# A scheduler's delays taken from the trace, and two batches' first-layer products by turns

## Chip, core and metric

The kernel runs on one core of a Trainium2 chip. The metric is the device time of one execution in microseconds. The engines: TensorE (PE) multiplies and, with an identity as one operand, transposes; VectorE (DVE), ScalarE (ACT) and GpSimd (POOL) work element by element; SyncE (SP) starts most transfers. [...]

## What is computed

```
# x: 8 batches, 8 heads, 512 tokens, 64;  state: 8, 8, 32, 64   (float32)
scores = x @ state^T / 8;   a  = softmax over the 32 states;   xread = a @ state
scores2 = state @ x^T / 8;  a2 = softmax over the 512 tokens;  sread = a2 @ x
y = concat([xread, sread], tokens)            # 8 x 544 tokens, heads side by side: 4352 rows of 512
h = y @ w_in                                  # w_in: 512 x 2048, float64
g = where(h > 0, h, exp(min(h, 0)) - 1)       # ELU
out = g @ w_out                               # w_out: 2048 x 512, float64
```

## The kernel before

All products are in float32. Three ideas matter here.

*Weights.* The weights arrive as 64-bit floats, in 32 blocks of 512 KB, sixteen for each layer. The chip makes 32-bit floats of them from the two words, with two passes on ACT and four on DVE for a block. The six buffers for raw blocks (`raws`) lie in the memory (`t_w_sb`) that later holds weight sums.

```python
def convert(dst, raw, pool_clamp=False, pool_add=False):
    lo, hi = words(raw)
    ...
    A.activation(out=lo.bitcast(FP32), in_=lo, func=AF.Copy, scale=2.0**-51, bias=2.0)
    A.activation(out=dst, in_=hi.bitcast(FP32), func=AF.Abs)
    (Q if pool_clamp else V).tensor_scalar(out=dst, in0=dst, ..., op0=ALU.max, op1=ALU.min)
    V.tensor_scalar(out=bits, in0=bits, scalar1=3, ..., op0=ALU.logical_shift_left)
    V.scalar_tensor_tensor(out=q, in0=hi, scalar=0x80000000, in1=lo, ...)
    (Q if pool_add else V).tensor_tensor(out=bits, in0=bits, in1=q, op=ALU.add)
```

*Order of work.* xread @ w_in is computed as a @ (state @ w_in). `make_m` is the inner product, for one of eight slices (`hc`) of w_in: 64 x 32 blocks of state times 256 columns of weights. `ffn1_plain` is the outer one, followed by the ELU: one ACT pass for exp, one for Relu, and one DVE operation. The converted slices of w_in are also stored in DRAM (`keep_w`); later batches fetch them again (`fetch`) into three buffers (`w_half`). The second layer, and for later batches the first too, use Strassen's scheme, whose sums of weights and of activations lie on DVE and POOL. `move_state` brings the second attention's weights into the form that `state_read` needs, with sixteen small transfers inside the chip's memory. `load_blocks` loads x of the next batch in blocks that DVE turns (`turn_blocks`).

```python
def start():
    ...
    load_states(0, 2, raw_s, (SP, ACT))
    load_x(0, (SP, ACT))
    ...
    for n in range(6):
        read_block(n)
    turn_states(raw_s, 0, 2)
    turn_x(ob)
    scores(0, ob)
    softmax(0, a_sb)
    for hc in range(8):
        for r in range(2):
            n = 2 * hc + r
            convert(*blocks[n])
            read_block(n + 6)
        ...
        make_m(0, hc, w)
        copy_m_half(0, hc, m_sb[:, c % 2])
        make_m(1, hc, w)
        dma(w_in_mem[:, hc], w, tokens=((), (f"mem{hc}",)), kind="keep_w")
        ...
        if hc == 2:
            turn_state()
            state_read(0)
            load_x(1)
            load_states(2, B, raw_t, (SP,))
            turn_states(raw_t, 2, B)
        if hc == 4:
            turn_x(ob)
            scores(1, ob)
            softmax(1, aT1)
            turn_state()
            state_read(1)
        if hc % 2:
            ffn1_plain(0, c, g0, a_sb, e_slots)
    for c in range(FC):
        ffn1_plain(1, c, g_sb, aT1, e_slots)
        for n in range(16 + 4 * c, 20 + 4 * c):
            convert(*blocks[n])
            if n + 6 < 32:
                read_block(n + 6)
    ...        # second layer of batch 0, then of batch 1; batches 2 to 7; the eight batches' sread rows
```

*The scheduler.* The code above runs no instruction at once: each call adds an operation, with an estimated cost, to a list. `Plan` then plays the list through, three times, against a model of the engines, [...]six rotating PSUM banks and the DMA queues. It keeps the order of its shortest pass, and the instructions of every engine are put out in that order. So the estimates set no time on the chip; they set the order. Where the model sees PE idle in the first 40 us, it puts in filler products of the identity, which keep PE running and whose result is used nowhere.

```python
class Plan:
    FREE_BANKS = 6
    LATENCY = {PE: 0.19, DVE: 0.07, ACT: 0.07, POOL: 0.09, SP: 0.0}
    ...
    def lag(self, a, b):
        return 0.0 if a.engine == b.engine and a.engine != SP else self.LATENCY[a.engine]
    ...
            _, n, op = heapq.heappop(heaps[e])       # PE: lowest number that is ready; others: earliest due
    ...
            if e == SP or op.moved:
                wire = max(wire, op.end) + op.moved / 260e3
                op.end = max(wire, op.end) + 1.9
...
def dma(out, in_, tokens=((), ()), queue=SP, kind="dma"):
    ...
    plan.add(
        queue, 0.06, issue(engine, "dma_start", dict(out=out, in_=in_)), [in_], [out],
        moved=size, tokens=tokens, name=kind,
    )
```

All instructions are put out by one helper (L410), so the profile tells them apart by tile and shape, not by line; the filler alone has its own line, L1341. In the tiles' names, `ps` is PSUM, `aT` the softmax weights, `m` the product of state and w_in, `g`, `sec` and `s` hold activations and their sums, `t_w` the raw blocks and then the weight sums, `xr` and `soft` the attention, `o` and `m` the output.

Of the kernel before, what the change touches and what calls it, by code (L numbers as in the profile page):

```python
# [76 lines left out]
class Op:  # L77
    __slots__ = (
        "number", "engine", "cost", "emit", "deps", "opens", "closes", "port", "moved", "start",
        "end", "due", "users", "name",  # L80
    )


class Plan:


    FREE_BANKS = 6
    LATENCY = {PE: 0.19, DVE: 0.07, ACT: 0.07, POOL: 0.09, SP: 0.0}
    WINDOW = 60

# [97 lines left out]
    def lag(self, a, b):  # L188
        return 0.0 if a.engine == b.engine and a.engine != SP else self.LATENCY[a.engine]

    def set_due(self, after):
        at = 0.0
        for op in self.ops:
            op.due = 1e6 + op.number
            if op.engine == PE:
                op.due = at
                at += op.cost
        follow = {}
        for a, b in after:
            follow.setdefault(a, []).append(b)  # L200
        for op in reversed(self.ops):
            took = op.cost
            if op.engine == SP:
                took = 2.0 + op.moved / 250e3
            for u in op.users:
                op.due = min(op.due, u.due - self.lag(op, u) - took)
            for u in follow.get(op, ()):
                op.due = min(op.due, u.due - self.lag(op, u) - took)

    def run(self, filler=None, until=0.0):  # L210
# [10 lines left out]
        next_bank, opened, port, wire = 0, 0.0, 0.0, 0.0  # L221
        holder, after, done, fills = {}, [], [], []
        left = [op for op in self.ops if op.engine == PE]
        lowest = 0

# [28 lines left out]
        while count < len(self.ops):  # L254
# [14 lines left out]
            if e == PE:  # L269
                while left and left[0] in scheduled:  # L270
                    left.pop(0)
                if heaps[e][0][1] > left[0].number + 1200:
                    assert pending[e] or True
            _, n, op = heapq.heappop(heaps[e])
            if op.port and port > at + 1e-9:
# [11 lines left out]
                heapq.heapify(heaps[e])  # L287
                op = x[2]
            op.start, op.end = at, at + op.cost
            if e == PE and filler and at < until:  # L290
                gap = op.start - free_at[PE]
# [18 lines left out]
            for b in self.closing.get(op, ()):  # L310
                if b.fixed is None:
                    lag = 0.0 if op.engine == PE else self.LATENCY[op.engine]
                    heapq.heappush(open_banks, (op.end + lag, b.index))
                    holder[b.index] = op
# [24 lines left out]
def kernel(  # L339
# [78 lines left out]
    class Engine:  # L418
# [3 lines left out]
        def __getattr__(self, name):  # L422
            def call(**kw):
# [5 lines left out]
                if self.key == DVE:  # L429
                    cost = 0.07 + 1.042 * n  # L430
                    alone = len(wide) == 1 and not isinstance(kw["out"], View)
                    if alone and name in ("tensor_scalar", "tensor_copy"):
                        cost, port = 0.07 + 0.65 * n, n > 0.1
                    port = port or len(wide) > 1
                elif self.key == ACT:
                    cost = 0.093 + 0.833 * n
                    cost += 0.09 * sum(is_ap(kw[k]) for k in ("scale", "bias") if k in kw)
                else:
                    cost = 0.1 + (2.45 if len(wide) > 1 else 1.85) * n
                    port = True  # L440
# [9 lines left out]
    def products(cost, calls, name="mm"):  # L450
# [15 lines left out]

        plan.add(PE, cost, emit, ins, outs, name=name)

    def turns(cost, calls, name="turn"):
# [9 lines left out]

        plan.add(PE, cost, emit, ins, outs, name=name)  # L480

# [30 lines left out]

    def x_tokens():
        return xe.rearrange("p (r c) -> p r c", r=R)

    def load_x(b, queues=(SP,)):
        x_v = x[b].rearrange("h (p r) d -> p r h d", r=R)
        for r in range(R):
            dma(
                x_tokens()[:, r].rearrange("p (h d) -> p h d", d=D), x_v[:, r],  # L520
                queue=queues[r % len(queues)], kind="load_x",
            )

    def load_blocks(b, raw):
# [16 lines left out]

    def turn_x(to):

        for i in range(2):
# [3 lines left out]
            for j in range(2):  # L548
                for r in range(R):
                    m = 2 * i + j  # L550
                    calls += turn_calls(
                        [v[t][:, j, r] for t in range(2)], x_tokens()[:, r, m * P : (m + 1) * P]
                    )
            turns(1.3, calls, "turn_x")
            o = to[:, i * 1024 : (i + 1) * 1024].rearrange(
# [5 lines left out]
    def load_states(b0, b1, raw, queues):  # L561
        for c in range(G):
            for m in range(NP):
                dma(
                    raw[m * NS : (m + 1) * NS, :, c], state_v[c, m, :, b0:b1],
                    queue=queues[(c * NP + m) % len(queues)], kind="load_states",
                )

    def turn_states(raw, b0, b1):
# [8 lines left out]
        turns(0.15 * n, calls, "turn_states")  # L578
        o = kT[:, b0:b1].rearrange("p b (t q) -> p t b q", t=2)
# [14 lines left out]
    def scores(b, xT):  # L594
        st[b, "s"] = ps = [bank(), bank()]
        by_state(
            b, ps, [xT[:, m * 512 : (m + 1) * 512] for m in range(NP)], slice(0, 512), 0.95,
            name="scores",
# [7 lines left out]
    def make_m(b, hc, w):  # L606
        c, h = divmod(hc, 2)
        if h == 0:
            st[b, "m", c] = [bank(), bank()]
        by_state(  # L610
            b, st[b, "m", c], [w[:, m] for m in range(NP)], slice(h * 256, (h + 1) * 256), 0.48,
            start=h == 0, name="make_m",
# [101 lines left out]

    def state_read(b):
        ps = bank()
        calls = []
        for g in range(G):
            for r in range(R):
                for m in range(NP):  # L720
                    calls.append((
                        ps[m * NS : (m + 1) * NS, g * D : (g + 1) * D],
                        read_weights()[:, g, r, m * NS : (m + 1) * NS],
                        x_tokens()[:, r, m * P + g * D : m * P + (g + 1) * D],
                        dict(start=r == 0, stop=r == R - 1, tile_position=(0, m * NS)),
                    ))
        products(1.1, calls, "state_read")
        for g in range(G):
# [306 lines left out]
    def start():  # L1035
# [3 lines left out]
        raw_s = g_flat[:, : 2 * P].rearrange("p (b c d) -> p b c d", b=2, c=G)  # L1039
        raw_t = g_flat[:, 2 * P : 8 * P].rearrange("p (b c d) -> p b c d", b=6, c=G)  # L1040
        m1 = [g_flat[:, (c + 1) * 2048 : (c + 1) * 2048 + 1024] for c in range(3)]
        m1.append(w_half[:, 2].rearrange("p m k -> p (m k)"))
        aT1 = s_buf[:, :1024]

        load_states(0, 2, raw_s, (SP, ACT))
        load_x(0, (SP, ACT))
        blocks = {}

# [3 lines left out]
        for n in range(6):  # L1052
            read_block(n)
        turn_states(raw_s, 0, 2)
        turn_x(ob)
        scores(0, ob)
        softmax(0, a_sb)
        for hc in range(8):
            for r in range(2):
# [8 lines left out]
            dma(w_in_mem[:, hc], w, tokens=((), (f"mem{hc}",)), kind="keep_w")  # L1068
            if hc % 2 == 0 or c < 3:
                copy_m_half(1, hc, m1[c] if c < 3 else None) if c < 3 else None  # L1070
            if hc == 7:
                copy_m(1, 3, m1[3])
            if hc == 2:
                turn_state()
                state_read(0)
                load_x(1)
                load_states(2, B, raw_t, (SP,))
                turn_states(raw_t, 2, B)
            if hc == 4:
                turn_x(ob)  # L1080
                scores(1, ob)
                softmax(1, aT1)
                turn_state()
                state_read(1)
            if hc % 2:
                ffn1_plain(0, c, g0, a_sb, e_slots)
        for c in range(FC):
            ffn1_plain(1, c, g_sb, aT1, e_slots)
            for n in range(16 + 4 * c, 20 + 4 * c):
                convert(*blocks[n])  # L1090
                if n + 6 < 32:
                    read_block(n + 6)
        n0 = Strassen(2, g0, [m_sb[:, i, :1024] for i in range(2)], s_buf)
# [27 lines left out]
        softmax(2, a_sb)  # L1121
        load_x(2)
        o.product(x1, o.s, t_w[1], False)
# [10 lines left out]
    def ffn2(o, b, x1=None):  # L1134
# [4 lines left out]
        if six:  # L1139
# [12 lines left out]
            if nxt:  # L1152
                softmax(b + 1, a_sb)
                load_x(b + 1)
                move_state()
# [61 lines left out]
    def turn_read():  # L1217
# [7 lines left out]
        turns(1.3, calls, "turn_read")  # L1225
        xT = st["xT"] = xr[:, :1024].rearrange("p (m b s) -> p m b s", m=NP, b=B)
# [156 lines left out]
```

## Time and profile before

| what | value |
|---|---|
| time, median of 3 runs | 754.21 us (752.23 to 756.72) |
| span of the profiled run | 752.6 us |
| PE, DVE, ACT, POOL busy | 96, 73, 39, 17% of the span |
| DMA moved | 78.52 MB, mean 104 GB/s |
| fetches of stored slices (512 KB) | 56, median 4.4 us from issue to landing |
| small moves for state_read (32 KB) | 96, median 1.9 us |
| x in blocks (64 KB) | 80, median 2.7 us |

A row of a group gives line, engine, operation, output and input tiles, shapes, how many, then busy time in us and mean ns of one, then the idle time before it and what ended it. A float32 product stands in the trace as two records. "SPq" is the issuing of a transfer by SyncE: while it lasts, nothing else on that queue is issued. The granted clock is 1.00 where TensorE runs at full speed.

### The profile page before, as it was taken

How to read it: one execution, taken by the hardware profiler on the slowest of the kernel's cores; microseconds unless marked ns; L12 is line 12 of the kernel's file. 1: busy time of each engine (PE TensorE's matmuls, PEld its weight loads, DVE VectorE, ACT ScalarE, POOL GpSimd, SP SyncE). 2: the span in 40 equal slices, each digit the busy share in tenths (PEclk: the TensorE clock that was granted, in tenths of full speed). 3: DMA queues.
4: the chain of work that ended last, by engine and by line, in shares of the span. 5: the costliest groups of instructions: out<-in, count | busy, mean ns of one | idle time of the engine just before them, and what ended most of it. 6: DMA issues, size and time to landing. Idle time of an engine off the chain costs nothing.

```text
span 752.6 us, 14169 instructions
## 1 busy us (share of the span) xinstructions
PE 725.4 (96%) x5608; PEld 593.3 (79%) x5608; DVE 548.7 (73%) x1030; ACT 295.6 (39%) x576; POOL 128.2 (17%) x158
## 2 busy tenths in 40 slices
PE   9998999999989989998999999998999899999998
PEld 7643458888968878787977888777978797899887
DVE  2997999998557956896858875895679684887231
ACT  4798991012056121732065213722074206610220
POOL 1101000042111150305130341107030522000000
PEclk9999999999999999999999999999999999999999
DMA  8797650223251343524172135324262323000401
GB/s 239 218 282 261 204 169 27 57 51 105 76 142 63 58 128 84 140 57 125 46 193 60 27 115 130 109 51 133 73 153 57 90 71 140 11 1 29 141 29 28
DMA packets 133442, 78.52 MB, mean 104 GB/s; under 512 B 114432, under 2 KB 114944, under 8 KB 133376
## 3 DMA queue, kind: packets, MB, share of 16 engines
q1 hardware_dynamic: 130880, 76.96, 36.4%
q10 hardware_dynamic: 2496, 0.66, 0.5%
q8 instruction: 44, 0.72, 0.4%
q14 instruction: 22, 0.18, 0.1%
HBM read 61.34 MB, written 13.11 MB: 99 GB/s over the span
## 4 chain that ended last, share of the span: by engine, by line
PE 64%; DVE 16%; DMA 8%; ACT 5%; SPq 4%; issue 2%; ACTq 0%; DVEq 0%
PE ps L410 63%; DVE g L410 6%; SPq L410 4%; DMA w_half<-w_in_mem 3%; DMA o<-in_x_dram 2%; ACT xe L410 2%; DVE sec L410 2%; DMA out_dram<-o 1%; DVE ps L410 1%; DVE s L410 1%; DVE xr L410 1%; DMA t_w<-in_moe_w_in_dram 1%; DVE xe L410 1%; DVE small L410 1%; PE ps L1341 1%
## 5 line engine op out<-in xcount | busy, mean ns | idle before, releaser
L410 PE MATMUL ps<-w_out,g 128*128 128x256 f32 (+1 forms) x960 | 173.3, 332 | 0.0
L410 PEld LDWEIGHTS ps<-w_out,g 128*128 128x128 f32 x960 | 150.1, 191 | 20.5 <-ACT o L410 4.2
L410 PE MATMUL ps<-aT,m 128*128 128x256 f32 (+1 forms) x568 | 156.4, 417 | 1.6 <-ACT sec L410 0.8
L410 PEld LDWEIGHTS ps<-aT,m 128*128 128x128 f32 x568 | 103.9, 192 | 42.4 <-issue 24.8
L410 DVE TENSOR_TENSOR o<-o,ps 128x128 f32<-128x128 f32 (+2 forms) x214 | 59.4, 287 | 75.3 <-PE ps L410 74.6
L410 POOL TENSOR_TENSOR soft<-soft,small 128x512 f32<-128x512 f32 x32 | 34.1, 1077 | 311.8 <-DVE small L410 233.4
L410 ACT ACTIVATE xe<-ps 128x512 f32<-128x512 f32 x104 | 59.8, 596 | 58.3 <-PE ps L410 41.3
L410 PE MATMUL ps<-sec 128*128 128x128 f32 x544 | 72.6, 276 | 2.4 <-DVE o L410 2.4
L410 POOL TENSOR_TENSOR m<-m 128x256 f32<-128x256 f32 x72 | 59.5, 841 | 64.6 <-ACT m L410 60.8
L410 PEld LDWEIGHTS ps<-sec 128*128 128x128 f32 x544 | 66.2, 192 | 5.1 <-DVE o L410 5.0
L410 PE MATMUL ps<-t_w,s 128*128 128x128 f32 (+1 forms) x448 | 70.1, 306 | 0.0
L410 PEld LDWEIGHTS ps<-t_w,s 128*128 128x128 f32 x448 | 63.0, 191 | 6.9 <-issue 2.5
L410 ACT COPY o<-ps 128x128 f32<-128x128 f32 (+2 forms) x55 | 21.9, 407 | 115.5 <-PE ps L410 109.2
L410 DVE SCALAR_TENSOR_TENSOR g<-xe,ps 128x512 f32<-128x512 f32 x56 | 38.1, 683 | 35.4 <-ACT xe L410 32.4
L410 ACT COPY m<-ps 128x512 f32<-128x512 f32 (+1 forms) x56 | 27.0, 527 | 79.0 <-PE ps L410 78.8
L410 PE MATMUL ps<-w_half,kT 64*32 64x256 f32 x1024 | 39.6, 385 | 15.0 <-DMA w_half<-w_in_mem 11.6
L410 ACT COPY ps<-ps 128x512 f32<-128x512 f32 x24 | 13.7, 572 | 94.6 <-PE ps L410 94.1
L410 PE MATMUL ps<-aT,s 128*128 128x256 f32 x168 | 42.2, 388 | 0.5 <-ACT sec L410 0.2
L410 POOL TENSOR_TENSOR s<-s 128x256 f32<-128x256 f32 x24 | 17.0, 727 | 135.2 <-ACT s L410 134.7
L410 DVE TENSOR_TENSOR ps<-sec,ps 128x512 f32<-128x512 f32 x48 | 33.2, 692 | 7.5 <-PE ps L410 4.8
L410 PEld LDWEIGHTS ps<-aT,s 128*128 128x128 f32 x168 | 30.5, 191 | 9.6 <-issue 2.4
L410 PEld LDWEIGHTS ps<-w_half,kT 64*32 64x32 f32 x1024 | 14.5, 105 | 29.4 <-DMA w_half<-w_in_mem 12.5
(108 smaller groups left out, 1078.8 us busy)
## 6 DMA issues: line engine op xcount, KB each, us to landing
w_half<-w_in_mem SPq DMA_DIRECT2D x56, 512.0 KB, 4.4
t_w<-in_moe_w_in_dram SPq DMA_DIRECT2D x16, 512.0 KB, 6.3
t_w<-in_moe_w_out_dram SPq DMA_DIRECT2D x16, 512.0 KB, 5.1
xe<-in_x_dram SPq DMA_DIRECT2D x30, 256.0 KB, 3.2
out_dram<-o SPq DMA_DIRECT2D x14, 512.0 KB, 2.6
o<-in_x_dram SPq DMA_DIRECT2D x80, 64.0 KB, 2.7
w_in_mem<-w_half SPq DMA_DIRECT2D x8, 512.0 KB, 7.4
xr<-xr SPq DMA_DIRECT2D x96, 32.0 KB, 1.9
```

What stands on the lines that cost most here:

```text
L410: ins = getattr(engine, name)(**{k: resolve(v) for k, v in kw.items()})
L1341: nc.tensor.matmul(psum[:, 7, :P], ident, ident, start=False, stop=True, skip_group_check=True)
```

## The change

It has two parts.

The model's numbers are replaced by durations from a trace. A hand-over now has a delay for each pair of engines, a transfer 2.2 us to land; an issue costs 0.44 or, for the small block transfers, 0.66 us; no more than eight transfers are under way at once; and costs of ACT, POOL and some DVE and PE operations are new. This is meant to order instructions as they become ready on the chip.

The start is rewritten. Batch 1's x is loaded early, into a place of its own, and both batches' attention is done before any first-layer product. Then the first-layer products of the two batches go by turns, one chunk each, behind every two slices of w_in; before, batch 1's all came after w_in. All second-layer blocks are converted after that in program order (the scheduler may move them). States are loaded with one transfer of 128 rows per batch and half of the heads instead of 32 rows with several batches, and the states of batches 2 to 7 are turned later.

```diff
-    LATENCY = {PE: 0.19, DVE: 0.07, ACT: 0.07, POOL: 0.09, SP: 0.0}
+    LAG = {
+        PE: {DVE: 0.21, ACT: 0.21, POOL: 0.25, SP: 0.3},
+        DVE: {PE: 0.15, DVE: 0.0, ACT: 0.12, POOL: 0.16, SP: 0.2},
+        ACT: {PE: 0.23, DVE: 0.14, ACT: 0.12, POOL: 0.18, SP: 0.2},
+        POOL: {PE: 0.12, DVE: 0.08, ACT: 0.08, POOL: 0.0, SP: 0.2},
+    }
+    LANDING = 2.2
...
+            if op.moved:
+                if len(lanes) >= 8:
+                    at = max(at, lanes[-8] + 0.1)
...
-                wire = max(wire, op.end) + op.moved / 260e3
-                op.end = max(wire, op.end) + 1.9
+                wire = max(wire, op.end) + op.moved / 250e3
+                op.end = wire + self.LANDING
+                lanes.append(op.end)
...
-                        cost, port = 0.07 + 0.65 * n, n > 0.1
+                        cost, port = 0.07 + 0.53 * n, n > 0.1
...
-                    cost = 0.093 + 0.833 * n
+                    cost = 0.055 + 0.84 * n
...
-            turns(1.3, calls, "turn_x")
+            turns(0.6, calls, "turn_x")
...
-            queue, 0.06, issue(engine, "dma_start", dict(out=out, in_=in_)), [in_], [out],
+            queue, 0.66 if kind in ("load_blocks", "move_state") else 0.44, issue(...), [in_], [out],
...
-        for c in range(G):
-            for m in range(NP):
+        for b in range(b0, b1):
+            for c in range(G):
                 dma(
-                    raw[m * NS : (m + 1) * NS, :, c], state_v[c, m, :, b0:b1],
+                    raw[:, b - b0, c], state_v[c, :, :, b],
...
+            if n == 3:
+                load_x(1, x_1)
         turn_states(raw_s, 0, 2)
-        turn_x(ob)
-        ...
-        for hc in range(8):
+
+        def w_step(hc):
             ...                      # convert, make_m for both batches, keep_w, copies, as before
+        def ffn1(c):
+            ffn1_plain(0, c, g0, a_sb, e_slots)
             ffn1_plain(1, c, g_sb, aT1, e_slots)
+        w_step(0)
+        turn_x(x_halves, ob)
+        scores(0, ob)
+        softmax(0, a_sb)
+        w_step(1)
+        turn_state()
+        state_read(0)
+        turn_x(x_1, ob)
+        scores(1, ob)
+        softmax(1, aT1)
+        turn_state()
+        state_read(1, x_1)
+        ffn1(0)
+        w_step(2)
+        w_step(3)
+        ffn1(1)
+        w_step(4)
+        load_states(2, B, raw_t, (SP,))
+        turn_states(raw_t, 2, B)
+        w_step(5)
+        ffn1(2)
+        w_step(6)
+        w_step(7)
+        ffn1(3)
+        for n in range(16, 32):
+            convert(*blocks[n])
+            if n + 6 < 32:
+                read_block(n + 6)
```

More of the change, by code (lines that the diff above doesn't have):

```diff
@@ L79 @@
         "number", "engine", "cost", "emit", "deps", "opens", "closes", "port", "moved", "start",
-        "end", "due", "users", "name",
+        "end", "due", "users", "name", "instr",
     )
@@ L87 @@
     FREE_BANKS = 6
-    LATENCY = {PE: 0.19, DVE: 0.07, ACT: 0.07, POOL: 0.09, SP: 0.0}
-    WINDOW = 60
+    LAG = {
[5 more added lines that the diff above has]
+    LANDING = 2.2
     def __init__(self, psum):
@@ L188, in lag @@
     def lag(self, a, b):
-        return 0.0 if a.engine == b.engine and a.engine != SP else self.LATENCY[a.engine]
+        if a.moved:
+            return 0.1
+        return self.LAG[a.engine].get(b.engine, 0.0)
     def set_due(self, after):
@@ L202, in set_due @@
             took = op.cost
-            if op.engine == SP:
-                took = 2.0 + op.moved / 250e3
+            if op.moved:
+                took = op.cost + self.LANDING + op.moved / 250e3
             for u in op.users:
@@ L221, in run @@
         next_bank, opened, port, wire = 0, 0.0, 0.0, 0.0
-        holder, after, done, fills = {}, [], [], []
-        left = [op for op in self.ops if op.engine == PE]
-        lowest = 0
+        holder, after, done, fills, lanes = {}, [], [], [], []
         def release(op):
@@ L268, in run @@
                 heapq.heappush(heaps[e], ((n if e == PE else op.due), n, op))
[L269 to L273, printed above, removed]
             _, n, op = heapq.heappop(heaps[e])
@@ L288, in run @@
                 op = x[2]
+            if op.moved:
+                if len(lanes) >= 8:
+                    at = max(at, lanes[-8] + 0.1)
             op.start, op.end = at, at + op.cost
             if e == PE and filler and at < until:
-                gap = op.start - free_at[PE]
                 t = free_at[PE]
@@ L311, in run @@
                 if b.fixed is None:
-                    lag = 0.0 if op.engine == PE else self.LATENCY[op.engine]
+                    lag = self.LAG[op.engine].get(PE, 0.0)
                     heapq.heappush(open_banks, (op.end + lag, b.index))
@@ L432, in call @@
                     if alone and name in ("tensor_scalar", "tensor_copy"):
-                        cost, port = 0.07 + 0.65 * n, n > 0.1
+                        cost, port = 0.07 + 0.53 * n, n > 0.1
                     port = port or len(wide) > 1
                 elif self.key == ACT:
-                    cost = 0.093 + 0.833 * n
-                    cost += 0.09 * sum(is_ap(kw[k]) for k in ("scale", "bias") if k in kw)
+                    cost = 0.055 + 0.84 * n
+                    cost += 0.1 * sum(is_ap(kw[k]) for k in ("scale", "bias") if k in kw)
+                    cost += 0.1 * ("accum_out" in kw)
                 else:
-                    cost = 0.1 + (2.45 if len(wide) > 1 else 1.85) * n
+                    cost = 0.06 + (1.86 if name == "tensor_tensor" and n > 0.3 else 2.45) * n
                     port = True
@@ L465, in emit @@
                 e()
-        plan.add(PE, cost, emit, ins, outs, name=name)
+        plan.add(PE, cost, emit, ins, outs, name=name).instr = 2 * len(calls)
     def turns(cost, calls, name="turn"):
@@ L478, in emit @@
                 e()
-        plan.add(PE, cost, emit, ins, outs, name=name)
+        plan.add(PE, cost, emit, ins, outs, name=name).instr = len(calls)
     def turn_calls(outs, in_):
@@ L493, in dma @@
         plan.add(
-            queue, 0.06, issue(engine, "dma_start", dict(out=out, in_=in_)), [in_], [out],
+            queue, 0.66 if kind in ("load_blocks", "move_state") else 0.44, issue(engine, "dma_start", dict(out=out, in_=in_)), [in_], [out],
             moved=size, tokens=tokens, name=kind,
@@ L511, in tops, with load_x @@
         return dict(top=t[:, 0:1], total=t[:, 1:2], top_t=t[:, 2:18], total_t=t[:, 18:34])
-    def x_tokens():
-        return xe.rearrange("p (r c) -> p r c", r=R)
-    def load_x(b, queues=(SP,)):
+    def load_x(b, to, queues=(SP,)):
         x_v = x[b].rearrange("h (p r) d -> p r h d", r=R)
@@ L519, in load_x, with x_rows @@
             dma(
-                x_tokens()[:, r].rearrange("p (h d) -> p h d", d=D), x_v[:, r],
+                x_rows(to, r).rearrange("p (h d) -> p h d", d=D), x_v[:, r],
                 queue=queues[r % len(queues)], kind="load_x",
             )
+    def x_rows(at, r):
+        return at[r // 2][:, r % 2 * DM : (r % 2 + 1) * DM]
+    x_halves = [xe[:, i * 1024 : (i + 1) * 1024] for i in range(2)]
     def load_blocks(b, raw):
@@ L540, in turn_blocks, with turn_x @@
             V.transpose(out=to[:, cols], in_=raw[:, cols])
-    def turn_x(to):
+    def turn_x(at, to):
         for i in range(2):
@@ L551, in turn_x @@
                     calls += turn_calls(
-                        [v[t][:, j, r] for t in range(2)], x_tokens()[:, r, m * P : (m + 1) * P]
+                        [v[t][:, j, r] for t in range(2)], x_rows(at, r)[:, m * P : (m + 1) * P]
                     )
-            turns(1.3, calls, "turn_x")
+            turns(0.6, calls, "turn_x")
             o = to[:, i * 1024 : (i + 1) * 1024].rearrange(
@@ L561, in load_states @@
     def load_states(b0, b1, raw, queues):
-        for c in range(G):
-            for m in range(NP):
-                dma(
-                    raw[m * NS : (m + 1) * NS, :, c], state_v[c, m, :, b0:b1],
-                    queue=queues[(c * NP + m) % len(queues)], kind="load_states",
+        for b in range(b0, b1):
+            for c in range(G):
+                dma(
+                    raw[:, b - b0, c], state_v[c, :, :, b],
+                    queue=queues[c % len(queues)], kind="load_states",
                 )
@@ L577, in turn_states @@
             )
-        turns(0.15 * n, calls, "turn_states")
+        turns(0.07 * n + 0.05, calls, "turn_states")
         o = kT[:, b0:b1].rearrange("p b (t q) -> p t b q", t=2)
@@ L596, in scores @@
         by_state(
-            b, ps, [xT[:, m * 512 : (m + 1) * 512] for m in range(NP)], slice(0, 512), 0.95,
+            b, ps, [xT[:, m * 512 : (m + 1) * 512] for m in range(NP)], slice(0, 512), 1.02,
             name="scores",
@@ L610, in make_m @@
         by_state(
-            b, st[b, "m", c], [w[:, m] for m in range(NP)], slice(h * 256, (h + 1) * 256), 0.48,
+            b, st[b, "m", c], [w[:, m] for m in range(NP)], slice(h * 256, (h + 1) * 256), 0.52,
             start=h == 0, name="make_m",
@@ L713, in move_state, with state_read @@
                 )
-    def state_read(b):
+    def state_read(b, at=x_halves):
         ps = bank()
@@ L723, in state_read @@
                         read_weights()[:, g, r, m * NS : (m + 1) * NS],
-                        x_tokens()[:, r, m * P + g * D : m * P + (g + 1) * D],
+                        x_rows(at, r)[:, m * P + g * D : m * P + (g + 1) * D],
                         dict(start=r == 0, stop=r == R - 1, tile_position=(0, m * NS)),
                     ))
-        products(1.1, calls, "state_read")
+        products(1.04, calls, "state_read")
         for g in range(G):
@@ L1039, in start @@
         raw_s = g_flat[:, : 2 * P].rearrange("p (b c d) -> p b c d", b=2, c=G)
-        raw_t = g_flat[:, 2 * P : 8 * P].rearrange("p (b c d) -> p b c d", b=6, c=G)
+        raw_t = xr[:, : 6 * P].rearrange("p (b c d) -> p b c d", b=6, c=G)
         m1 = [g_flat[:, (c + 1) * 2048 : (c + 1) * 2048 + 1024] for c in range(3)]
         m1.append(w_half[:, 2].rearrange("p m k -> p (m k)"))
+        x_1 = [g_flat[:, (c + 2) * 2048 + 1024 : (c + 3) * 2048] for c in range(2)]
         aT1 = s_buf[:, :1024]
         load_states(0, 2, raw_s, (SP, ACT))
-        load_x(0, (SP, ACT))
+        load_x(0, x_halves, (SP, ACT))
         blocks = {}
@@ L1053, in start @@
             read_block(n)
+            if n == 3:
+                load_x(1, x_1)
         turn_states(raw_s, 0, 2)
-        turn_x(ob)
-        scores(0, ob)
-        softmax(0, a_sb)
-        for hc in range(8):
+        def w_step(hc):
             for r in range(2):
@@ L1068, in start @@
             dma(w_in_mem[:, hc], w, tokens=((), (f"mem{hc}",)), kind="keep_w")
-            if hc % 2 == 0 or c < 3:
-                copy_m_half(1, hc, m1[c] if c < 3 else None) if c < 3 else None
-            if hc == 7:
+            if c < 3:
+                copy_m_half(1, hc, m1[c])
+            elif hc == 7:
                 copy_m(1, 3, m1[3])
[L1073 to L1087, printed above, removed]
-            ffn1_plain(1, c, g_sb, aT1, e_slots)
[L1089 to L1092, printed above, removed]
+        def ffn1(c):
+            ffn1_plain(0, c, g0, a_sb, e_slots)
+            ffn1_plain(1, c, g_sb, aT1, e_slots)
+        w_step(0)
[26 more added lines that the diff above has]
+                read_block(n + 6)
         n0 = Strassen(2, g0, [m_sb[:, i, :1024] for i in range(2)], s_buf)
@@ L1121, in start @@
         softmax(2, a_sb)
-        load_x(2)
+        load_x(2, x_halves)
         o.product(x1, o.s, t_w[1], False)
@@ L1153, in ffn2 @@
                 softmax(b + 1, a_sb)
-                load_x(b + 1)
+                load_x(b + 1, x_halves)
                 move_state()
@@ L1224, in turn_read @@
             )
-        turns(1.3, calls, "turn_read")
+        turns(0.66, calls, "turn_read")
         xT = st["xT"] = xr[:, :1024].rearrange("p (m b s) -> p m b s", m=NP, b=B)
```

## The prediction

> **What bounds the kernel now.** I read the page's busy shares first, then TensorE's waits, the group of its filler products, its timeline, and last the queues and engines that feed it.
>
> ```profile
> PE 725.4 (96%) x5608; PEld 593.3 (79%) x5608; DVE 548.7 (73%) x1030; ACT 295.6 (39%) x576; POOL 128.2 (17%) x158
> ```
>
> TensorE (PE) is the bound: whatever the schedule does, it pays only through the 4% in which PE has no product, and through PE work that is not part of the result. Both have a row. The waits of PE (total us, times, longest):
>
> ```profile
> PE ps L410 <- DMA w_half<-w_in_mem: 11.6, 5, 2.8
> PE ps L410 <- DVE o L410: 2.4, 5, 0.6
> PE ps L410 <- ACT soft L410: 2.0, 1, 2.0
> PE ps L410 <- DVE g L410: 2.0, 1, 2.0
> PE ps L410 <- POOL ident masks.py:199: 1.4, 1, 1.4
> ```
>
> With four smaller rows (1.3, 1.0, 0.9, 0.8) they sum to 23.4 us. The span is 752.6, so 752.6 - 725.4 - 23.4 = 3.8 us are left: the tail behind the last product. Half of the waiting is one kind, the fetch of a stored weight slice (w_half from w_in_mem), once in each of five batches. The groups of instructions give the filler:
>
> ```profile
> L1341 PE MATMUL ps<-ident 128*128 128x128 f32 x168 | 20.7, 282 | 0.0
> ```
>
> These identity products only keep PE running. Each product is two records, so there are 84, at 20.7 / 84 = 0.246 us. They all lie ahead of 40 us: PE is starved at the start. Its timeline shows how long that stage is, and the idle 2.02 us in it:
>
> ```profile
> 62.66 0.66 PE L410 MATMUL ps<-ident,soft 128*128 128x128 f32 x4 [2.02 <-ACT soft L410]
> 108.23 13.98 PE L410 MATMUL ps<-w_out,sec 128*128 128x256 f32 x64
> 135.86 7.07 PE L410 MATMUL ps<-t_w,s 128*128 128x256 f32 x32
> ```
>
> The second layer starts at 108.23; its first product with a weight sum (t_w) at 135.86. In the table by stretches (columns after the span: PE, PE load, DVE, ACT and POOL busy, then the granted clock) a wait of 2 us costs more than itself:
>
> ```profile
> 62.70:66.00 3.30, 3.30 (x9) 1.54 (x10) 3.30 (x7) 2.21 (x5) 0.00 (x0) 0.68 0.32 125
> 222.50:228.00 5.50, 5.48 (x42) 3.70 (x43) 3.12 (x6) 2.77 (x5) 0.68 (x1) 0.69 0.63 226
> ```
>
> Behind the waits that end at 62.66 and 222.52 PE is busy but slow: 0.31 x 5.5 = 1.7 us lost in the second, about as much in the first (clock 0.84 in the next 4 us too). That is 3.4 us hidden in "busy".
>
> Why the fetch is late, from SyncE's timeline:
>
> ```profile
> 256.98 11.74 SPq L410 DMA_DIRECT2D xr<-xr  x16
> 268.81 5.22 SPq L410 DMA_DIRECT2D w_half<-w_in_mem  x4
> ```
>
> PE used that slice's buffer for the last time at 258.1, but the fetch stands behind sixteen small moves (move_state), each holding the queue 11.74 / 16 = 0.73 us. The data land 4.07 us later, and PE starts at 272.92 after 2.79 us idle. The kernel's scheduler took an issue to cost 0.06 us, so to it the sixteen were free.
>
> [...]
>
> **The change part by part.** No product, conversion or activation is added or removed; the counts by engine are the same but for filler and DMAs. So I keep a ledger of PE: span = useful work + filler + waits + tail. Useful work is 725.4 - 20.7 = 704.7, or 701.3 without the two half-clock stretches. The order of instructions is fixed when the program is built, so the changed order can be read; only its times are unknown.
>
> *Filler.* The changed program holds 74 fillers: 74 x 0.246 = 18.2 us, 2.5 less.
>
> *Start.* Up to 108.23 PE had 20.7 us of filler and 5.6 of waits (1.36, 0.44, 1.33, 0.45, 2.02), so 81.9 of useful work. The same with the new filler and the first 1.4 us is 81.9 + 18.2 + 1.4 = 101.5, plus new waits. Attention of both batches now precedes the first-layer products, which then run 8 by 8 (batch 0, batch 1) with make_m between: 14.2 us of products cover two slices' conversion, where before batch 1's 27.8 us stood in one piece behind all of w_in. It can only work if VectorE (DVE) keeps up. Three blocks convert in 5.62 us:
>
> ```profile
> 120.37 1.09 DVE L410 TENSOR_SCALAR w_out<-w_out 128x512 f32<-128x512 f32 x3
> 121.38 1.89 DVE L410 SCALAR_TENSOR_TENSOR t_w<-t_w 128x512 uint32<-128x512 uint32 x3
> 123.18 1.09 DVE L410 TENSOR_SCALAR w_out<-w_out 128x512 uint32<-128x512 uint32 x3
> 124.19 1.89 DVE L410 CUSTOM_DVE_ANT_0 w_out<-w_out,t_w 128x1024 uint16<-128x1024 uint16 x3
> ```
>
> that is 1.87 each. Ahead of the first t_w product DVE's new order has 32 blocks (59.8), 32 ELU operations at 0.60 from start to start (19.2), two softmaxes of some 7.2 (14.4), 11 sums of 1024 at 1.14 (12.5) and about 4 of small things: 110 us. Its first operation comes when PE has run 25 fillers behind the identity products, near 5.1 + 6.1 = 11.2 us, so it is through at 121 plus its own idle time. PE is there at 101.5 + 27.6 = 129.1. DVE may idle 8 us. Before, it idled 9.7 us between 20 and 130 (ten minus its busy time, from a table by 10 us). So the margin is thin, and ACT, about 16 of every 16.4 us busy in the interleaved stretch (16 ELU passes at 0.57, copies, conversions), has no more. I put 3 us of waits here.
>
> *Queue order.* In the new order two fetches go ahead of the sixteen moves, and the slice that PE waited for is requested right behind the product that frees its buffer; 11 pieces of second-layer work (some 0.9 us each) and one make_m follow before it is needed, 10 us against a landing of 4 to 5. I take the 11.6 us as gone. Both stores now go ahead of the loads of the next x blocks, 14 of which stand behind one fetch; at 0.66 each (five took 3.31 on SyncE before) they end, by my count of the products ahead, some 50 us after a batch's small Strassen steps begin, and the next scores need them near 69. State loads of 128 rows each (2 per queue ahead of the first weights, not 4) free SyncE's queue earlier.
>
> *Hand-overs.* PE's other waits from 200 to 650 us are 18.1 - 11.6 = 6.5 us (idle time from a table by 25 us). Delays nearer to the trace should place those better, and new ones will arise: 5 us.
>
> *Sum.* 701.3 + 18.2 + 1.4 + 3.8 = 724.7; waits 3 + 5; one half-clock stretch 1.7: span 734.4. A run takes 1.8 us more than its span (754.44 against 752.6): **736.2**; I say **736.5**.
>
> **Rivals.** (1) *DVE or ACT becomes the bound of the start.* For it: both were over 90% busy from 80 to 110. If DVE idles 12 us ahead of the t_w sums, as its two softmaxes in a row, which have almost no conversion between them, might make it, PE waits 4 us and loses clock: 742 or so. Against it: its work is the same and begins at about the same time (10.6 before). (2) *The fetch wait moves.* The moves now wait for two fetches and are themselves needed by state_read; or PE waits for x blocks. At 1 to 2 us in six batches: 745. [...] Against it: the slacks above, 5 and some 19 us. (3) *Everything fits:* 4 us of waits in all and full clock, 730. (4) *The schedule is not obeyed:* the new delays are wrong [...] (the first state loads held a queue 1.5 us each) and all that was saved comes back as waits: 750.
>
> **Range and chances.** 2% faster is 739.1, which allows 12.6 us of waits and lost clock over 726.5; I expect 9.7. The spread of my waits is some 6 us, so 0.6 for faster. Slower by 2% would need 43 us of waits, twice what there is now: 0.02. Range 729 (rival 3) to 747 (a little beyond rival 2).
>
> **What would show it.** Right: filler near 18 us; the row of PE waiting for w_half gone or under 3 us; second layer starting at 102 to 106; PE busy about 720; no half clock near 222. Wrong: a new row of PE waiting for w_half, g or w_out ahead of 130 us (rival 1), or for xr or o after 200 (rival 2), or PE busy falling by less than the filler. What would break the ledger is useful work that itself grows[...].

## The result, and the profile after

The changed kernel takes 726.45 us (725.68 to 727.12), against 755.47 for the kernel before on the same chip: a ratio of 0.961, 95% interval 0.956 to 0.967. That is 29 us less where the forecast had 18, and below the range of 729 to 747. Part of it is clock: 31 executions of the kernel before took 750.6 to 760.4 us while their mean granted clock fell from 0.998 to 0.986, four of the changed kernel 725.7 to 727.1 at 0.999 to 1.0. At the old kernel's median clock of 0.993 that is an estimated 0.007 x 755 = 5 us of the 29; the profile on which the ledger rests, with 0.995, holds 3.4.

The page of the changed kernel, first its busy shares, then TensorE's waits (total us, times, longest):

```profile
PE 712.2 (98%) x5588; PEld 594.0 (82%) x5588; DVE 544.9 (75%) x1030; ACT 292.4 (40%) x576; POOL 131.3 (18%) x158
```

```profile
PE ps L413 <- DVE o L413: 3.5, 10, 0.4
PE ps L413 <- POOL ident masks.py:199: 1.4, 1, 1.4
PE ps L413 <- DVE w_out L413: 0.8, 1, 0.8
PE ps L413 <- ACT read L413: 0.7, 1, 0.7
PE ps L413 <- DVE ps L413: 0.5, 1, 0.5
PE ps L413 <- DVE g L413: 0.4, 1, 0.4
PE ps L413 <- ACT m L413: 0.2, 1, 0.2
```

They sum to 7.5 us, where it was 23.4. The fetch of w_half, 11.6 us before, is gone from the list. The filler's group:

```profile
L1361 PE MATMUL ps<-ident 128*128 128x128 f32 x148 | 19.1, 281 | 0.0
```

PE's timeline, at the start of the second layer, its one wait there, the first weight sum, and batch 2's first product:

```profile
101.54 8.80 PE L413 MATMUL ps<-w_out,sec 128*128 128x256 f32 x40
111.14 5.45 PE L413 MATMUL ps<-w_out,sec 128*128 128x256 f32 x24 [0.80 <-DVE w_out L413]
...
130.24 7.07 PE L413 MATMUL ps<-t_w,s 128*128 128x256 f32 x32
...
201.91 1.89 PE L413 MATMUL ps<-aT,m 128*128 128x256 f32 x8
```

In the kernel before, batch 2's first product stood at 207.55:

```profile
207.55 4.81 PE L410 MATMUL ps<-aT,m 128*128 128x256 f32 x20
```

This row is a good place to cut. Ahead of it the change saved 207.55 - 201.91 = 5.6 us. Behind it lie 752.6 - 207.55 = 545.1 us before and 723.9 - 201.91 = 522.0 after: 23.1 us. So four fifths of the gain come from batches 2 to 7, of which the change rewrites no line of work, only the order.

How the order of one queue changed is seen on SyncE's timeline, in the stage where the fetch stood behind sixteen small moves before:

```profile
246.55 0.82 SPq L413 DMA_DIRECT2D w_half<-w_in_mem  x2
250.22 11.08 SPq L413 DMA_DIRECT2D xr<-xr  x16
261.40 1.10 SPq L413 DMA_DIRECT2D w_half<-w_in_mem  x2
```

The sixteen moves still hold the queue for 11 us. Two fetches now go ahead of them, and PE works on through the whole stage.

In this profile the granted clock stays at full speed from the first record, at 4.2 us, to the end of the products; the two half-clock stretches are gone. In the profile of before they lie at 63.9 and 224.3 us, 3.41 us each at a clock of 0.50: eight records of 256 columns take 3.68 us from 224.14, where eight take 1.89 at 201.91 in the changed kernel. Half of each is lost, 3.4 us in all, as the forecast had it.

### The profile page after: what moved, and what is told of

Its sections match the earlier page's. It is cut to its first block, busy times and chain, and to the rows that moved or that the text cites. A ratio compares the mean times of both kernels' runs of the same rounds, so it can differ in the third digit from the quotient of the medians.

```text
span 723.9 us, 14101 instructions
## 1 busy us (share of the span) xinstructions
PE 712.2 (98%) x5588; PEld 594.0 (82%) x5588; DVE 544.9 (75%) x1030; ACT 292.4 (40%) x576; POOL 131.3 (18%) x158
## 4 chain that ended last, share of the span: by engine, by line
PE 61%; DVE 29%; issue 3%; ACT 3%; POOL 2%; DMA 1%; SPq 1%; DVEq 0%; POOLq 0%; ACTq 0%
PE ps L413 60%; DVE g L413 7%; DVE sec L413 4%; DVE s L413 4%; DVE small L413 3%; DVE t_w L413 1%; POOL soft L413 1%; DVE w_out L413 1%; DVE ps L413 1%; DVE soft L413 1%; DVE o L413 1%; ACT xe L413 1%; DVE xr L413 1%; DVE m L413 1%; PE ps L1361 1%
## 5 line engine op out<-in xcount | busy, mean ns | idle before, releaser
L413 PE MATMUL ps<-aT,m 128*128 128x256 f32 (+1 forms) x568 | 148.4, 407 | 1.2 <-ACT read L413 0.7
L413 PEld LDWEIGHTS ps<-aT,m 128*128 128x128 f32 x568 | 105.7, 190 | 32.6 <-issue 16.6
L413 POOL TENSOR_TENSOR m<-m 128x256 f32<-128x256 f32 x72 | 57.0, 810 | 192.4 <-ACT m L413 191.0
L413 DVE TENSOR_SCALAR xe<-xe 128x512 f32<-128x512 f32 x48 | 20.4, 431 | 27.7 <-ACT xe L413 27.5
L413 ACT COPY sec<-ps 128x512 f32<-128x512 f32 x48 | 28.0, 584 | 22.4 <-PE ps L413 22.2
```

Source lines behind the costliest of these rows:

```text
L413: ins = getattr(engine, name)(**{k: resolve(v) for k, v in kw.items()})
```

## The ledger against the measurement

| part of the span, us | forecast | measured |
|---|---|---|
| useful products (busy less filler) | 701.3 | 693.1 |
| filler | 18.2 | 19.1 |
| first wait | 1.4 | 1.4 |
| other waits | 3 + 5 | 6.1 |
| half-clock stretch | 1.7 | 0 |
| remainder (the forecast's "tail") | 3.8 | 4.2 |
| span | 734.4 | 723.9 |

The waits were nearly right. The largest error is in the term that I had taken as fixed: the same products were 8.2 us shorter in "busy". A kernel that computes the same thing can't do less useful work, so before, some of what counts as busy was waiting. (The last row isn't all tail: in both traces the last product ends 3.45 us before the span does, and the rest is gaps of under 0.15 us, too short for the list of waits.)

It can be found from the trace by the start of each product. For every kind of full-size product (128 rows by 128) I took the time to the next one's start, subtracted that kind's median (0.216 us for one record of 256 columns), and sorted what was left over. From batch 2 on:

| left over by one product | before | after |
|---|---|---|
| 0.015 to 0.15 us | 178 times, 15.5 us | 101 times, 9.6 us |
| 0.15 to 0.3 us | 13 times, 2.6 us | once, 0.2 us |
| over 0.3 us | 12 times, 17.6 us | 6 times, 2.9 us |

The sum falls by 23 us, the whole gain of these batches; at products of other shapes what is left over adds up to about 30 us both before and after. The first row is 5.9 us of it, and none of that is in PE's list of waits. The reason lies in the records: one of 256 columns lasts 0.38 us, and the next starts 0.216 us after its start. So a record covers the first 0.16 us of any stall behind it, and a short stall whole. Of the middle row of before, 8 records and 1.75 us lie in the half-clock stretch at 224.3. One row of waits shows short stalls where PE loads weights. Before and after:

```profile
PEld ps L410 <- ACT sec L410: 6.3, 19, 0.8
```

```profile
PEld ps L413 <- ACT sec L413: 0.9, 3, 0.4
```

## Experiments

The theory after the comparison: the price of an issue made the queue's order and removed the fetch wait; the hand-over delays removed the short stalls; the new order of work gave the 5.6 us at the start. The rivals: one part alone does it all, or the new start makes the later batches run well. Times are medians. "Start" is the time up to batch 2's first product and "rest" the span behind it, both in the one profiled execution. That execution was 4.7 us above the median for "old transfers alone" and 2.6 above it for "before, with new transfers". The changed kernel was profiled twice: its start was 201.9 and 202.9 us, its rest 522.0 and 521.9, so differences of 1 us in a start say nothing.

| kernel | time, us | start | rest | short stalls in rest |
|---|---|---|---|---|
| before | 754 to 756 | 207.6 | 545.1 | 178 |
| changed | 726.5 | 201.9 | 522.0 | 101 |
| old start, new durations | 737.3 | 212.9 | 522.5 | 103 |
| new start, old durations | 750.5 | 204.2 | 544.5 | 200 |
| old transfers alone | 754.6 | 204.4 | 553.1 | 135 |
| old price of an issue alone | 737.2 | 201.3 | 534.6 | 127 |
| old hand-overs alone | 738.3 | 207.5 | 528.3 | 173 |
| two of the hand-overs old | 731.3 | 202.6 | 527.1 | 150 |
| old costs alone | 725.6 | 202.0 | 521.9 | 134 |
| before, with new transfers | 738.1 | 212.3 | 526.6 | 181 |
| without filler | 726.9 | 203.0 | 522.2 | 101 |
| longer hand-overs | 730.6 | 203.3 | 525.5 | 107 |

### The two parts apart

The old start under the new durations:

```diff
 def start():
-    ...   # attention of both batches first, products by turns, states by 128 rows
+    ...   # the body and the state loads of the kernel before
```

> The changed kernel with the start of the kernel before (its order of work and its state loads), all new durations kept. Theory A: the two parts add up, and the start is worth what the traces show ahead of the second layer: 108.23 - 101.54 = 6.7 us, so 733 us, and the batches stay free of fetch waits. Rival B: the new durations alone repair the old start too (its order is the model's choice), and this is within 2 us of 726.5. Rival C: the start's new order is what makes the batches run well, and this is above 740.

It takes 737.33 us, ratio to before 0.978 (0.974 to 0.983). None of the three numbers holds. The rest is 522.5 us, as in the changed kernel, so rival C falls: the batches don't need the new start. But the start itself is 11 us longer than the new one and 5 longer than the old one under the old durations. PE's rows at the beginning of the second layer say where:

```profile
109.45 11.39 PE L413 MATMUL ps<-w_out,sec 128*128 128x256 f32 x52
122.96 4.54 PE L413 MATMUL ps<-w_out,sec 128*128 128x256 f32 x12 [2.13 <-DVE w_out L413]
...
141.16 7.07 PE L413 MATMUL ps<-t_w,s 128*128 128x256 f32 x32
```

The second layer starts 7.9 us later than in the changed kernel and 1.2 later than before; 92 fillers instead of 74 are part of that. The first weight sum comes 31.7 us after the second layer starts, against 27.6 before and 28.7 in the changed kernel: PE waits 2.13 us for a block that DVE has not converted, and the 12 records behind it take 4.54 us, where 12 at 0.216 from start to start take 2.8. This is the prediction's rival 1, in a kernel where it was not looked for.

The new start under the old durations, all of the model's numbers set back:

```diff
-    LAG = {...}
+    LATENCY = {PE: 0.19, DVE: 0.07, ACT: 0.07, POOL: 0.09, SP: 0.0}
...      # landing, limit of eight and all costs of operations likewise
-            queue, 0.66 if kind in ("load_blocks", "move_state") else 0.44, issue(...)
+            queue, 0.06, issue(...)
```

> The changed kernel with every duration of the scheduler's model as before, and the new start kept. Theory A: the 23 us that the batches gained come back, the start keeps about 4 of its 6.7: 748 to 750 us, with some 11 us of PE waiting for w_half. Rival C: the new start does most of it, 735 or less. A third way: the new start under the old durations is worse than the old one, above 755.

750.53 us, 0.994 of before (0.991 to 0.996), as theory A had it. The start keeps 3.4 us of its gain, the batches lose nearly everything (544.5 us, after 545.1 before and 522.0), and PE waits as before:

```profile
PE ps L408 <- DMA w_half<-w_in_mem: 10.6, 5, 3.1
```

So the new order of work alone is worth 4 to 6 us (3.9 between the profiled executions, 5.7 between the medians), and together with the new durations 11 (737.3 to 726.5). The durations alone are worth some 17 to 19, and 24 with the new order. The parts don't simply add.

### Transfers, hand-overs, costs

One group of the model's numbers at a time was set back in the changed kernel. First the transfers:

```diff
-            return 0.1
+            return 0.0
...
-            if op.moved:
-                took = op.cost + self.LANDING + op.moved / 250e3
+            if op.engine == SP:
+                took = 2.0 + op.moved / 250e3
...
-                if len(lanes) >= 8:
+                if False:
...
-                wire = max(wire, op.end) + op.moved / 250e3
-                op.end = wire + self.LANDING
+                wire = max(wire, op.end) + op.moved / 260e3
+                op.end = wire + 1.9
...
-            queue, 0.66 if kind in ("load_blocks", "move_state") else 0.44, issue(...)
+            queue, 0.06, issue(...)
```

> The changed kernel, with only the model's transfers as before: an issue costs 0.06 us, landing 1.9, no limit of eight under way. Theory D (the price of an issue makes the queue's order, which removes the fetch wait): PE waits 8 to 12 us for w_half again, time 736 to 740, while stalls of under 0.15 us stay at about 100. Rival E (the delays of the hand-overs do it): no wait for w_half, under 730.

754.55 us: no faster than before (1.000, 0.997 to 1.003). Theory D had the wait for w_half about right (7.9 us) and the total wrong by 15. The profiled execution had a mean granted clock of 0.986, an estimated 0.014 x 757.5 = 10.6 us lost, and three more waits grew:

```profile
PE ps L413 <- DMA w_half<-w_in_mem: 7.9, 5, 2.2
PE ps L413 <- DVE g L413: 7.3, 5, 3.8
PE ps L413 <- ACT o L413: 3.2, 5, 0.6
PE ps L413 <- DVE ps L413: 3.0, 9, 0.6
```

The rest, 553 us in this execution, is longer than with every number old (544.5); at the median, 4.7 us lower, it would still be some 3 to 4 us longer. My reading, which no run shows, is that a model with right hand-overs and free issues makes a plan that is tighter and can't be kept.

Within the transfers, the price of an issue alone:

```diff
-            queue, 0.66 if kind in ("load_blocks", "move_state") else 0.44, issue(...)
+            queue, 0.06, issue(...)
```

> The changed kernel with only the price of an issue as before, 0.06 us; landing 2.2 and the limit of eight under way stay. Theory D (the price of the issue is what mattered among the transfers' numbers): PE waits 6 to 10 us for w_half and some for x blocks (g, ps), time 742 to 755. Rival G (landing time and the limit do it): no wait for w_half, under 732.

737.18 us (0.976 of before, 0.975 to 0.978): 10.7 more than the changed kernel, between the two theories. The expected wait did not come back; another arose:

```profile
PE ps L413 <- DMA xr<-xr: 6.9, 4, 2.4
```

SyncE's timeline, in the same stage as above:

```profile
246.15 5.86 SPq L413 DMA_DIRECT2D xr<-xr  x9
252.11 0.54 SPq L413 DMA_DIRECT2D w_half<-w_in_mem  x1
252.70 5.77 SPq L413 DMA_DIRECT2D xr<-xr  x7
```

With the other numbers of the transfers new, the fetch is put among the moves in time, so PE need not wait for it though issues are free. But the moves come late: with free issues the scheduler seems to call for their data before the sixteen can have been issued. So 10.7 of the 28 us that the transfers' numbers are worth go with the price of the issue. The rest goes with landing time and limit of eight, together with the smaller numbers changed beside them (250 GB/s instead of 260, 0.1 us behind a landing). These free the fetch; no run sets them apart, and none has the new price of an issue without them.

The other way round, the transfers' numbers alone added to the kernel before:

```diff
+        if a.moved:
+            return 0.1
...
-            if op.engine == SP:
-                took = 2.0 + op.moved / 250e3
+            if op.moved:
+                took = op.cost + 2.2 + op.moved / 250e3
...
+                if len(lanes) >= 8:
+                    at = max(at, lanes[-8] + 0.1)
...
-                wire = max(wire, op.end) + op.moved / 260e3
-                op.end = max(wire, op.end) + 1.9
+                wire = max(wire, op.end) + op.moved / 250e3
+                op.end = wire + 2.2
+                lanes.append(op.end)
...
-            queue, 0.06, issue(...)
+            queue, 0.66 if kind in ("load_blocks", "move_state") else 0.44, issue(...)
```

> The kernel before, with only the model's transfers as in the changed one (issue 0.44 or 0.66 us, landing 2.2, eight under way); old start, old hand-overs, old costs. Theory D: the fetch wait (11.6 us) and the half clock behind 222 us are gone, batches and tail 545 to about 530 us; with a start like the old one 738 to 744. Rival H (the transfers pay only where the hand-overs are right too, as two wrong sets spoiled each other the other way round): 748 or more.

738.05 us (0.979, 0.976 to 0.981), as theory D had it: the rest falls to 526.6, with no wait for the fetch of w_half, and the short stalls stay at 181. That is 18.5 of the 23.1 us that the batches gain in all, from the transfers' numbers alone. The start is 4.7 us longer than before in this execution. Its mean granted clock is 0.995, an estimated 0.005 x 738.9 = 3.7 us lost, much as in the profile of before (3.4); how much of that lies in the start was not shown. The old start does not gain from the new numbers, here as above.

Now the hand-overs:

```diff
-    LAG = {PE: {DVE: 0.21, ...}, DVE: {PE: 0.15, ...}, ACT: {PE: 0.23, ...}, ...}
+    LATENCY = {PE: 0.19, DVE: 0.07, ACT: 0.07, POOL: 0.09, SP: 0.0}
```

> The changed kernel, with only the hand-over delays as before (one for each engine: PE 0.19, DVE and ACT 0.07, POOL 0.09). Theory D: no wait for w_half; the short stalls of PE inside what counts as busy go from about 100 back to some 180 in the batches, 5 to 6 us, and the waits of 0.3 us and more for DVE, ACT grow by 1 to 3: 732 to 735. Rival E: 738 or more, with fetch waits. Rival F: the schedule hardly feels 0.1 us, within 1 us of 726.5.

738.29 us (0.979, 0.975 to 0.984). In the batches theory D held in its main point: no wait for w_half, 173 short stalls worth 15.2 us (5.7 more), the rest 6.3 us longer. The longer waits there hardly grew (4.2 us after 4.0), where it had 1 to 3 more. What I had not expected is another 5.6 us in the start, with 3.2 of them a wait for w_out. The weight loads wait for ACT as often as before the change:

```profile
PEld ps L408 <- ACT sec L408: 5.7, 20, 0.4
```

Then only the two delays of data that come to PE:

```diff
-        DVE: {PE: 0.15, ...},
-        ACT: {PE: 0.23, ...},
+        DVE: {PE: 0.07, ...},
+        ACT: {PE: 0.07, ...},
```

> The changed kernel, with two delays alone as before: from DVE to PE and from ACT to PE, 0.07 us instead of 0.15 and 0.23. Theory: these two are what the short stalls come from (PE's weight loads stand ready for data that the model took to be there 0.1 us earlier), so the short stalls in the batches go from 101 to 150 or more, 4 to 6 us, and the batches and tail from 522 to 526 or more: 731 to 738. Rival: the delays on the way from PE, or to SyncE and POOL, make the difference, and this is within 2 us of 726.5.

731.32 us, 4.8 more than the changed kernel beside it. Short stalls rise to 150 (by 4.2 us), the rest to 527.1, and the row is back; the wait for the output sums grows too, from 3.5 us:

```profile
PEld ps L413 <- ACT sec L413: 4.9, 16, 0.4
PE ps L413 <- DVE o L413: 6.6, 6, 1.3
```

Two numbers, wrong by 0.08 and 0.16 us, cost 5 us. With all hand-overs old, 5.7 us of short stalls came back; so these two account for most of it.

The costs of the operations themselves, on all engines:

```diff
-                        cost, port = 0.07 + 0.53 * n, n > 0.1
+                        cost, port = 0.07 + 0.65 * n, n > 0.1
...
-                    cost = 0.055 + 0.84 * n
+                    cost = 0.093 + 0.833 * n
...
-            turns(0.6, calls, "turn_x")
+            turns(1.3, calls, "turn_x")
...  # PE's other products and GpSimd's operations likewise
```

> The changed kernel with only the costs of operations as before (ACT, POOL, the one-source DVE operations, turns and packed products). Theory: they differ from the new ones by less than 0.1 us each, except the turns, so 727 to 732, without fetch waits; rival: every set of numbers is needed, 738 or more, with short stalls of PE back at 170 or so.

725.63 us (725.19 to 725.79): no loss, and with the changed kernel at 726.54 (725.62 to 726.84) no difference that I would call one. The short stalls rise to 134 while the stalls over 0.3 us nearly vanish (0.4 us); the sum is the same. So a number of short stalls says little by itself; what counts is the sum of all stalls. New costs were not needed. It is the fastest kernel of the study, by less than can be told apart.

### Filler and margins

```diff
-    steps, fills = plan.order(3, fill, 40.0)
+    steps, fills = plan.order(3, None, 40.0)
```

> The changed kernel without the 74 filler products; all other instructions in the same order. Theory P (the filler lies in time in which PE would idle and only keeps its clock): 18 us of new idle time ahead of 34 us, half clock for parts of the first 40 us, second layer 2 to 8 us later than 101.5, time 729 to 734. Rival Q (filler stands in the way of products that are ready): second layer at 97 to 100, time 722 to 725. Rival R (neither): within 1 us of 726.5.

726.90 us (0.963 of before, 0.962 to 0.965): rival R. The second layer starts at 102.67. In the two profiles of the changed kernel it starts at 101.54 and 102.57, so this is no shift. The filler's 19 us become waits for some 11 (18.4 us in all, after 7.5), while the useful products take 9.5 us longer, as many at the start run slower. The longest new wait, and the stretch from 20 to 30 us (clock 0.67):

```profile
PE ps L413 <- DMA g<-in_state_dram: 4.8, 2, 4.6
20.00:30.00 10.00, 7.20 (x80) 4.19 (x80) 9.11 (x24) 7.26 (x19) 3.40 (x4) 0.67 1.03 366
```

Between those products PE waits for DVE, ACT or a transfer anyway, so their slowness is hidden. The filler buys nothing here that can be told from the spread.

The changed kernel as it is, measured once more, beside one with longer delays between PE, DVE and ACT:

> The changed kernel itself, so that the two beside it, and the runs without filler and with the old costs, have a neighbour on the same chip: 725.5 to 727.5 us.

```diff
-        PE: {DVE: 0.21, ACT: 0.21, ...}, DVE: {PE: 0.15, ...}, ACT: {PE: 0.23, ...}
+        PE: {DVE: 0.29, ACT: 0.29, ...}, DVE: {PE: 0.25, ...}, ACT: {PE: 0.33, ...}
```

> A candidate: the changed kernel with some 0.1 us added to the delays between PE, DVE and ACT (0.29 from PE, 0.25 and 0.33 to PE). If a schedule that believes in late data is the safer one, the short stalls fall under 80 and PE's waits for the output sums (3.5 us) go: 721 to 725. If the delays were right already, operations are only put off, within 1 us of 726.5; if they are too long, idle time that was not needed: 728 or more.

The changed kernel again took 726.54 us; with longer delays it takes 730.55 (729.83 to 731.17), ratios to before 0.962 (0.958 to 0.966) and 0.967 (0.964 to 0.971). The candidate fails. Short stalls are no fewer (107), the wait for the output sums stays, and a new one comes up:

```profile
PE ps L413 <- DVE o L413: 3.2, 9, 0.6
PE ps L413 <- DMA xr<-xr: 2.8, 2, 1.5
```

So errors of some 0.1 us in these pairs cost 4 to 5 us on either side: the delays of the change are right to within that.

## Why the prediction was right or wrong

**Right: the start.** The ledger had 101.5 plus waits, and the second layer began at 101.54. The new waits up to there were 0.71, 0.22 and 0.44, 1.4 in all; with the 0.8 for w_out behind it that is 2.2 of the 3. They fit in because the 81.9 us still held the half-clock stretch of the old start, which is gone. That the two numbers agree so closely is luck: in the second profile of the same kernel the layer began at 102.57.

**Nearly: DVE's margin.** PE reached the first weight sum at 130.24 (forecast 129.1 plus waits), with 0.8 us of waiting for w_out. DVE was indeed the neighbour of the bound: in the stretches from 40 to 140 us it is busy for 98%.

```profile
40.00:100.00 60.00, 59.33 (x321) 25.99 (x320) 59.06 (x112) 56.65 (x115) 0.79 (x1) 1.00 0.84 260
100.00:140.00 40.00, 39.20 (x178) 33.42 (x178) 39.25 (x57) 13.26 (x24) 0.00 (x0) 1.00 0.20 66
```

Rival 1 did not happen here, but in the old start under the new durations (2.1 us for w_out) and under the old hand-overs (3.2) it did.

**Right: the fetch.** The 11.6 us went, by the queue order read from the changed program. The runs correct the reason. The prediction laid the wait to issues that the scheduler took to be free; but in the changed kernel with issues free again, and the other numbers of the transfers new, the fetch was not late; the moves were (6.9 us).

**Right: the clock**, and too cautious by one stretch of 1.7 us. ("Tail", 3.8 us, was a remainder: the tail is 3.45, the rest short gaps.)

**Wrong: the hand-overs.** The step that failed is "PE's other waits are 6.5 us ... 5 us", together with "useful work is 701.3". I took the list of PE's waits to hold all of its waiting. It left out stalls of under 0.15 us, 15.5 us of them from batch 2 on. The new delays cut these by 5.9, which I had booked as useful work that can't change; the same products came to 693.1 us of "busy", 8.2 less. Setting all hand-overs back brought 5.7 us of the short stalls back, two of them alone 4.2. The listed waits other than the fetch also fell further, to 4.0 us from batch 2 on.

The remaining 2.3 us of the 8.2 no experiment assigns. Some 0.4 lie ahead of batch 2. About 0.7 are the part of longer waits that the record ahead covers: each takes 0.16 to 0.37 us more from start to start than its row says (the fetch at 272.92 has 2.79 in its row and 2.95 above the median from start to start), and from batch 2 on there are 11 such waits instead of 15. The rest stays open.

**Wrong in kind: filler as a cost.** I credited 2.5 us for ten fillers fewer. Without any filler the time is the same within 1 us. Filler stood in time in which PE could not have gone on, so fewer of them save nothing by themselves.

**Rivals 2 and 4** were real dangers: set back one group of numbers and waits come up elsewhere (w_half, g, xr), with the transfers' numbers to the point of losing everything. In the batches the new transfers alone kept them away, with every other number old (rest 526.6, no row of waiting for a fetch or a move).

## What to carry to other kernels

A schedule made from a model is worth what its worst number is worth: a plan with the transfers' old numbers lost 28 us, and errors of some 0.1 us in two hand-overs cost 5 us of 726. Price what occupies a queue (here sixteen issues of 32 KB held SyncE's for 11.7 us), not only what crosses the wire, and look again at which wait takes the place of the one removed. In an engine that is 96% busy, measure stalls also by the time between starts against the median for the same shape, because short ones are counted as work (15.5 us of them here).

## What was not expected of the hardware

In the changed kernel an issue on SyncE of a 32 KB move within the chip's memory takes 0.61 us in the median of 96, of a 512 KB fetch 0.36 in the median of 56 (single ones up to 1.5 and 1.6): here the larger transfer has the shorter issue. Of the waits of about 2 us in the kernel before, those of 2.02 and 1.98 us were followed by a half-clock window of 3.41 us, 1.2 and 1.8 us after they ended; the five for the fetch, of 1.8 to 2.8 us, were not. The profile's first clock record comes some microseconds after the start, at 4.2 us in the changed kernel. In the run without filler 16 records of the scores at 15.01 took 2.44 us, against 1.14 in the changed kernel at 15.17, 2.1 times as long, although the table says 1.00 for the stretch from 10 to 20 us: so in that stretch its 1.00 is no proof of full speed.
